# Transposing by DMA through DRAM instead of on the TensorE, in a kernel that gates two attention branches

## The chip, the cores and the metric

One core of a Trainium2 chip. The metric is the device time of one execution in microseconds (us). PE is TensorE, PEld its weight loads, DVE VectorE, ACT ScalarE, POOL GpSimd, and SP the engine that issues the DMAs. L12 is line 12 of the kernel that is being talked about, so the same statement has different line numbers in different kernels.

## The reference, cut to what matters

The input x has 2048 rows of 640. The output is `g * a + (1 - g) * b`, where g is a sigmoid of x times a vector, and a and b are two attention branches with 32 heads of 20.

```python
# branch A: linear attention; phi_k, phi_q are softmaxes of k, q times a small matrix
kv = einsum('bhsf,bhsd->bhfd', phi_k, v);  z = einsum('bhsf->bhf', phi_k)
a = (einsum('bhqf,bhfd->bhqd', phi_q, kv) / den) @ A_wo
# branch B: four segments of 512 rows; softmax attention inside a segment, memory M of earlier ones
logits = einsum('bhqd,bhkd->bhqk', qs, ks) * scale + mask
a_dot  = einsum('bhqk,bhkd->bhqd', softmax(logits), vs)
o = g * a_mem + (1 - g) * a_dot
b = o @ B_wo
```

## The kernel before

The matmuls of this kernel contract over the partition axis of both operands, so three things have to stand transposed: x (for all projections), k of branch B (for the scores) and both branches' outputs (for the last matmuls). The kernel before does each on PE, as a matmul with an identity, into one of four shared PSUM buffers, and DVE copies it out.

```python
psw = ctx.enter_context(tc.tile_pool(name="psw", bufs=4, space=PSUM))   # the four shared buffers
...
def x_transpose(sc):                      # 16 chunks of 128 rows
    tp = wtile("xtp", BF16)               # a shared PSUM buffer
    for c in range(KC):                   # KC = 5
        nc.tensor.transpose(out=tp[:, c * P:(c + 1) * P],
                            in_=x_nat[sc // 4][:, sc % 4, c * P:(c + 1) * P], identity=ident_b)
    nc.vector.tensor_copy(out=xT[:, :, sc * P:(sc + 1) * P], in_=...)
...
def b_kT(s, g):                           # segment s, group g of four heads: 32 times
    ps = wtile("kT_ps", BF16)
    for c in range(4):
        nc.tensor.transpose(out=ps[:, c * P:(c + 1) * P],
                            in_=kpad2[s % 2][:, c, 4 * g:4 * g + 4, :], identity=ident_b)
    kT = bw.tile([P, L], BF16, name="kT", bufs=2)
    nc.vector.tensor_copy(out=kT, in_=ps[:, 0:L])
    return kT
...
def fin_tr(s, qc, X):                     # X = 0: A's output, 1: B's; 32 times
    tp = wtile("otp", BF16)
    ...                                   # five transposes, one DVE copy to oT
def fin_mm(s, qc, hf):                    # ten matmuls oT x Wo, an ACT copy, at hf = 1 a DMA out
```

The kernel has three stages: branch A's keys and state over 16 chunks; a loop over 4 x 8 groups of heads; and a tail for the last segment's outputs. In the loop, a group's score matmuls (`st`), their exponentials on ACT (`PT`), and the previous group's value matmuls (`nd_ps`) are joined by filler units: next segment's k and v, branch A's outputs, and the output matmuls of earlier segments. Each unit has a fixed place in PE's order, given in groups:

```python
for s, (p0, p1) in enumerate(((9.01, 17), (17.01, 25), (25.4, 32))):   # output units of segment s
    fill += place(fill_fin(s), ((0, p0), (1, p1)))
```

The softmax here doesn't subtract the row's maximum and nothing guards it: scores larger than these inputs give would overflow.

## Time and profile before

| | before |
|---|---|
| median time, 16 executions | 438.92 us (436.54 to 441.15) |
| PE busy, share of the profiled span | 364.8 us of 436.2 us, 84% |
| ACT, DVE, POOL busy | 63%, 60%, 48% |
| loop, from the first to the last score matmul | 101.6 to 412.3 us |

First the page of the profiled execution before: the span; busy time, share and instruction count of each engine; the TensorE clock in tenths of full speed in 40 slices; the DMA totals; and the shares of the chain of work that ended last.

```profile
span 436.2 us, 10502 instructions
...
PE 364.8 (84%) x4289; PEld 234.1 (54%) x4289; DVE 260.2 (60%) x680; ACT 274.8 (63%) x515; POOL 210.6 (48%) x365
...
PEclk9999999999899798699999999899999997998669
...
DMA packets 10610, 12.49 MB, mean 29 GB/s; under 512 B 1347, under 2 KB 10563, under 8 KB 10563
...
PE 51%; ACT 19%; DVE 15%; POOL 9%; issue 4%; DMA 2%; POOLq 0%; SPq 0%; DVEq 0%; ACTq 0%
```

PE leads: it has the largest busy share and half of the chain. But the chain also passes through ACT, DVE and POOL, so PE is not the only thing that matters. Next, busy time of each engine in two stretches: ten microseconds of the first stage, and the whole loop. After the five busy times come the mean granted TensorE clock, the DMA share and GB/s.

```profile
core 0: us, PE busy (x) PEld busy (x) DVE busy (x) ACT busy (x) POOL busy (x), PEclk, DMA share, GB/s
40.00:50.00 10.00, 10.00 (x143) 8.24 (x142) 6.93 (x11) 5.84 (x17) 8.65 (x12) 1.00 0.01 3
101.60:412.30 310.70, 259.09 (x3112) 153.57 (x3114) 183.30 (x533) 216.89 (x365) 142.82 (x253) 0.93 0.02 7
```

In the first stage PE is busy without a gap. In the loop it is busy 259 of 310.7 us. In the 51.6 us that are left PE does nothing; most of that is waits. The clock is 0.93 on average. Next, the groups of the transposes and of one of the copies (busy us and mean ns after the first bar; then the idle time just before them and what ended it), and two rows of the timeline: five transposes' weight loads, and those of the next five matmuls.

```profile
L415 DVE COPY kT<-kT_ps 128x512 bf16<-128x512 bf16 x32 | 13.3, 416 | 0.9 <-PE kT_ps L412 0.9
...
L412 PE MATMUL kT_ps<-ident_b,kpad 128*128 128x128 bf16 x128 | 12.7, 221 | 1.8 <-DVE ts L538 0.9 <-ACT eq L401 0.9
...
L210 PE MATMUL xtp<-ident_b,x_nat 128*128 128x128 bf16 x80 | 8.0, 242 | 9.7 <-DVE xT L213 5.1 <-DMA x_nat<-in_A_x_dram 4.7
L551 PE MATMUL otp<-ident_b,oB 128*128 128x128 bf16 x80 | 7.8, 229 | 4.7 <-POOL oB L491 1.8 <-ACT eq L401 1.8 <-DVE ts L538 0.9
...
L551 PE MATMUL otp<-ident_b,oA 128*128 128x128 bf16 x80 | 7.6, 230 | 0.0
```

```profile
43.56 0.40 PEld L210 LDWEIGHTS <-x_nat 128*128 128x128 bf16 x5
...
43.92 0.36 PEld L184 LDWEIGHTS <-wnat_q 128*120 128x120 bf16 x5
```

One transpose is recorded as 220 ns long, but five of them take 43.92 - 43.56 = 0.36 us of PE's issue, 72 ns each, because they are pipelined. So busy time and issue time of the same instructions differ.

### The profile page before, as it was taken

To read this page: it belongs to the slowest core of one execution; us is meant where nothing else is said; L and a number is where in the kernel's file an instruction comes from. 1 tells how busy PE (TensorE), PEld (TensorE's weight loads), DVE (VectorE), ACT (ScalarE), POOL (GpSimd) and SP (SyncE) were. 2 spreads that over 40 slices of the span, in tenths; PEclk is the share of its full clock that TensorE was granted. 3 is DMA by queue.
4 is the path that set the end of the run, shared out by engine and by line. 5 is a ranking of instruction groups with operands and counts; after the bars stand their busy time and mean duration, and the time that the engine had idled before them with its cause. 6 is when DMAs were issued, how large, how long until landed. Compare 5 with 4: busy or idle time off the path is not lost.

```text
span 436.2 us, 10502 instructions
## 1 busy us (share of the span) xinstructions
PE 364.8 (84%) x4289; PEld 234.1 (54%) x4289; DVE 260.2 (60%) x680; ACT 274.8 (63%) x515; POOL 210.6 (48%) x365
## 2 busy tenths in 40 slices
PE   1899999797987687888988798898887788878686
PEld 1677877673544353455655465564554454445354
DVE  5378766795367454577666557565666556555431
ACT  1576666526687477677776776586675886676502
POOL 9037877860255434444453434454354544446510
PEclk9999999999899798699999999899999997998669
DMA  8961000000000000000000000000000000000001
GB/s 251 363 198 36 5 2 2 2 0 2 2 2 1 2 2 0 2 2 2 17 9 9 17 15 4 2 17 2 17 16 2 17 2 17 17 2 15 17 12 50
DMA packets 10610, 12.49 MB, mean 29 GB/s; under 512 B 1347, under 2 KB 10563, under 8 KB 10563
## 3 DMA queue, kind: packets, MB, share of 16 engines
q1 hardware_dynamic: 10563, 11.83, 8.3%
q8 instruction: 33, 0.54, 0.5%
q14 instruction: 14, 0.11, 0.1%
HBM read 9.21 MB, written 2.62 MB: 27 GB/s over the span
## 4 chain that ended last, share of the span: by engine, by line
PE 51%; ACT 19%; DVE 15%; POOL 9%; issue 4%; DMA 2%; POOLq 0%; SPq 0%; DVEq 0%; ACTq 0%
ACT PT L434 12%; PE o_ps L565 10%; PE pq_ps L500 6%; PE qb_ps L393 5%; PE st L428 4%; PE va_ps L231 4%; PE vb_ps L231 4%; PE nd_ps L448 4%; POOL PT L438 3%; PE kb_ps L231 3%; PE ka_ps L231 3%; DVE ts L538 2%; PE acc L271 2%; ACT eq L401 2%; PE otp L551 2%
## 5 line engine op out<-in xcount | busy, mean ns | idle before, releaser
L434 ACT ACTIVATE PT<-st 128x1024 bf16<-128x1024 f32 (+1 forms) x192 | 158.9, 885 | 21.0 <-PE st L428 18.7
L438 POOL TENSOR_SCALAR_AFFINE_SELECT PT<-PT 128x512 bf16<-128x512 bf16 x128 | 80.5, 641 | 113.4 <-ACT PT L434 97.8
L231 PEld LDWEIGHTS <-xT 128*128 128x128 bf16 x640 | 61.1, 99 | 31.6 <-issue 6.8
L428 PE MATMUL st<-qT,kT 32*128 32x128 bf16 (+3 forms) x512 | 44.6, 312 | 15.3 <-ACT PT L434 13.1
L397 DVE CAST qT<-qb_ps 128x512 bf16<-128x512 f32 x32 | 22.1, 692 | 45.6 <-PE qb_ps L393 45.6
L259 POOL TENSOR_TENSOR EkN<-Ek,krec 128x1280 bf16<-128x1280 bf16 x16 | 37.8, 2363 | 20.1 <-DVE krec L258 17.9
L448 PE MATMUL nd_ps<-vB,PT 128*128 128x21 bf16 x1280 | 42.5, 174 | 5.4 <-DVE ts L538 2.0
L448 PEld LDWEIGHTS <-PT 128*128 128x128 bf16 x1280 | 38.2, 96 | 11.7 <-POOL rr L529 3.8
L543 POOL TENSOR_TENSOR oA<-ts 128x360 bf16<-128x360 f32 (+1 forms) x32 | 27.5, 860 | 31.6 <-DVE ts L538 28.1
L393 PE MATMUL qb_ps<-xT,WqB 128*128 128x512 bf16 x160 | 41.7, 393 | 0.9 <-DVE ts L538 0.8
L500 PE MATMUL pq_ps<-xT,WqA 128*128 128x512 bf16 x120 | 35.0, 429 | 6.7 <-DVE ts L538 3.1
L565 PEld LDWEIGHTS <-oT 128*128 128x128 bf16 x320 | 31.6, 104 | 15.8 <-issue 1.7
L569 ACT CAST osb<-o_ps 128x320 bf16<-128x320 f32 x32 | 13.6, 425 | 40.1 <-PE o_ps L565 39.9
L428 PEld LDWEIGHTS <-kT 32*128 32x128 bf16 x512 | 14.0, 92 | 42.4 <-issue 37.1
L503 ACT ACTIVATE Eq<-pq_ps 128x512 bf16<-128x512 f32 x24 | 14.3, 597 | 29.4 <-PE pq_ps L500 29.2
L565 PE MATMUL o_ps<-WoA,oT 128*128 128x320 bf16 x160 | 30.2, 324 | 2.1 <-DVE ts L538 1.4
L518 PE MATMUL num_ps<-KVZ,Eq 128*128 128x132 bf16 (+1 forms) x192 | 18.5, 220 | 13.7 <-DVE ts L538 5.5
L231 PE MATMUL vb_ps<-WvB,xT 128*128 128x320 bf16 x160 | 26.5, 313 | 3.7 <-DVE ts L538 2.3
L565 PE MATMUL o_ps<-WoB,oT 128*128 128x320 bf16 x160 | 29.5, 319 | 0.0
L538 DVE TENSOR_TENSOR ts<-num_ps,cs 128x360 f32<-128x360 f32 (+1 forms) x64 | 28.2, 483 | 1.9 <-DVE cs L533 0.2
L241 ACT CAST vA<-va_ps 128x320 bf16<-128x320 f32 x32 | 13.6, 425 | 22.8 <-PE va_ps L231 22.8
L251 ACT ACTIVATE Ek<-ka_ps 128x320 bf16<-128x320 f32 x64 | 23.0, 440 | 5.5 <-PE ka_ps L231 4.9
(114 smaller groups left out, 667.0 us busy)
## 6 DMA issues: line engine op xcount, KB each, us to landing
out_dram<-osb SPq DMA_DIRECT2D x16, 160.0 KB, 1.8
x_nat<-in_A_x_dram SPq DMA_DIRECT2D x3, 640.0 KB, 8.9
WvA<-in_A_wqkv_dram SPq DMA_DIRECT2D x1, 800.0 KB, 5.3
wnat_k<-in_A_wqkv_dram SPq DMA_DIRECT2D x1, 800.0 KB, 7.0
wnat_q<-in_A_wqkv_dram SPq DMA_DIRECT2D x1, 800.0 KB, 11.0
WkB<-in_B_wk_dram SPq DMA_DIRECT2D x1, 800.0 KB
WvB<-in_B_wv_dram SPq DMA_DIRECT2D x1, 800.0 KB, 11.2
wq_st<-in_B_wq_dram SPq DMA_DIRECT2D x5, 160.0 KB, 7.7
```

The lines of the kernel that those rows point to most:

```text
L231: nc.tensor.matmul(ps, lhsT=xT[:, c, sc * P:(sc + 1) * P], rhs=W[:, c, lo:hi], start=(c == 0), stop=(c == KC - 1))
L251: nc.scalar.activation(out=Ek[:, sgn, 320 * hf:320 * hf + 320], in_=ps[:, 0:320], func=ACT.Exp, scale=1.0 if sgn == 0 else -1.0)
L259: nc.gpsimd.tensor_tensor(out=EkNs[sc % 4][:, 0:1280].rearrange("p (h f) -> p h f", f=DH), in0=Ek.rearrange("p s (h f) -> p (s h) f", f=DH ...
L393: nc.tensor.matmul(ps, lhsT=WqB[:, c, 4 * g:4 * g + 4, :], rhs=xT[:, c, s * L:(s + 1) * L], start=(c == 0), stop=(c == KC - 1))
L428: nc.tensor.matmul(st2[i // 2][:, i % 2, o:o + n], lhsT=kT[r:r + 32, c * P:(c + 1) * P], rhs=qT[r:r + 32, c * P:L], start=True, stop=True, ...
L434: nc.scalar.activation(out=PT[:, 2 * pr:2 * pr + 2, base:base + w], in_=st2[pr][:, :, 0:w], func=ACT.Exp, scale=SCALE_B)
L438: nc.gpsimd.affine_select(out=view, in_=view, pattern=[[0, 4], [1, P]], compare_op=ALU.is_ge, fill=0.0, base=0, channel_multiplier=-1)
L448: nc.tensor.matmul(nd[:, j * 84 + i * V1:j * 84 + (i + 1) * V1], lhsT=PT[:, i, o:o + P], rhs=vb[:, c, 4 * g + i, :], start=(j == 0 and i = ...
L500: nc.tensor.matmul(ps, lhsT=WqA[:, c, g * 120:g * 120 + P], rhs=xT[:, c, s * L:(s + 1) * L], start=(c == 0), stop=(c == KC - 1))
L538: nc.vector.tensor_tensor(out=ts[:, sgn, 0:nh, :], in0=pss[sgn][:, :, 0:DH], in1=cs[:, sgn, 0:nh, None].to_broadcast([P, nh, DH]), op=ALU. ...
L543: nc.gpsimd.tensor_tensor(out=segs[s].oA[:, qc, h0 * DH:(h0 + nh) * DH].rearrange("p (h d) -> p h d", d=DH), in0=ts[:, 0, 0:nh, :], in1=ts ...
L565: nc.tensor.matmul(ps[:, 0:320], lhsT=segs[s].oT[qc, X][:, k5 * P:(k5 + 1) * P], rhs=Wo[:, k5, hf * 320:hf * 320 + 320], start=(n == 0), s ...
```

## The change

Its intent is to take transposes off PE and their copies off DVE, and to use the DMA engines, which do almost nothing after the loads (share 0.01 to 0.02 above). Chunks 8 to 15 of x come by a transposing DMA straight from the input. k and the outputs are written to DRAM and read back by a transposing DMA. Only the last segment's B outputs stay on PE, as they would be waited for. Every one of these DMAs is issued by SP. The output units of each segment also start later in the loop, by 0.4 to 0.8 group. The core of the diff:

```diff
+    dram = ctx.enter_context(tc.tile_pool(name="dram", bufs=1, space=bass.MemoryType.DRAM))
+    kd = [dram.tile([L, H * 32], BF16, name=f"kd{s}") for s in range(NSEG)]
+    od = [[dram.tile([L, D], BF16, name=f"od{s}_{X}") for X in range(2)] for s in range(NSEG)]
...
-    for i in range(1, 4):
-        nc.sync.dma_start(out=x_nat[i], in_=xv[:, 4 * i:4 * i + 4, :])
+    nc.sync.dma_start(out=x_nat[1], in_=xv[:, 4:8, :])
     wload(wnat_q, A_wqkv[:, 0:D])
     wload(WkB, B_wk)
     wload(WvB, B_wv)
...                                              (five loads of B_wq, now into five buffers, not two)
+    for sc in range(8, NCH):
+        nc.sync.dma_start_transpose(out=xT[:, :, sc * P:(sc + 1) * P],
+                                    in_=x2[sc * P:(sc + 1) * P, :])
     wload(WoA, A_wo)
     wload(WoB, B_wo)
     nc.sync.dma_start(out=beta_b, in_=B_beta.partition_broadcast(P))
...                                              (in b_k: kpad is now three rotating tiles)
+        rows = slice(c * P, (c + 1) * P)
+        nc.sync.dma_start(out=kd[s][rows, :], in_=kp.rearrange("p h d -> p (h d)"))
+        nc.sync.dma_start_transpose(out=kT2[s % 2][:, :, rows], in_=kd[s][rows, :])
...                                              (b_kT is gone)
+    def o_put(s, X, qc, src):
+        nc.sync.dma_start(out=od[s][X][qc * P:(qc + 1) * P, :], in_=src)
+    def o_get(s, X, qc):
+        rows = slice(qc * P, (qc + 1) * P)
+        oT = bw.tile([P, KC, P], BF16, name=f"oT{X}", bufs=4)
+        nc.sync.dma_start_transpose(out=oT, in_=od[s][X][rows, :])
+        segs[s].oT[qc, X] = oT
...
-    for s, (p0, p1) in enumerate(((9.01, 17), (17.01, 25), (25.4, 32))):
-        fill += place(fill_fin(s), ((0, p0), (1, p1)))
+    for s, (p0, p1) in enumerate(((9.8, 17.2), (17.8, 25.2), (25.8, 32))):
+        fin = place(fill_fin(s), ((0, p0), (1, p1)))
+        fill += fin
+        for X in range(2):
+            fill += [(max(fin[2 * qc][0] - 0.8, 8 * s + 8.7),
+                      lambda s=s, X=X, qc=qc: o_get(s, X, qc)) for qc in range(4)]
```

## The prediction

> What bounds the kernel now. The page gives PE 364.8 us of 436.2 us (84%), ACT 63%, DVE 60%, POOL 48%. By windows there are three stages. From 20 to 80 us (branch A) PE is busy 9.5 to 10.0 us of every 10: it alone is the limit. From 100 to 400 us (the loop over 32 head groups) PE is busy 85 to 89%, ACT about 70%, DVE about 64%; the chain of work that ended last hops between PE matmuls, the ACT exponentials into PT and some DVE and POOL steps. PE leads, with small waits on others. The last 20 us are one chain: epilogue, transposes, output matmuls. DMA is nearly idle after 45 us.
>
> What the change removes. PE transposes: 40 of x (chunks 8 to 15), all 128 of k, 140 of 160 of the outputs: 308 of 4289 matmuls. By the groups of instructions these are 4.0 + 12.7 + 13.5 = 30 us of PE busy time. In the timeline five transposes in a row start 72 ns apart, so as issue time they are 308 x 72 ns = 22 us: 3 us in the PE-bound first stage, 19 us later. Also removed: copies out of PSUM on DVE, 8 x 0.49 + 32 x 0.42 + 28 x 0.49 = 31 us of DVE's 260 us, and 68 uses of the four shared PSUM buffers.
>
> What it adds. 44 writes to DRAM (160 to 256 KB) and 52 transposing DMAs, all issued by SP. In the trace a 160 KB output write lands in 1.8 us; it has no transposing DMA. The Trainium skill, "Advanced Engine Details and Errata", section "X-Bar Transpose (TRN2)", says that transposing DMAs on trn2 are as fast as regular ones; no run here shows that yet. My estimate is 2 us each, with 4 us allowed for. A write and its transpose are then 4 to 6 us of latency, in a queue that waits in order. The traffic is spread over 300 us. ACT and POOL work is unchanged.
>
> Critical path. k and A's outputs have lead times of several to tens of us (one group lasts about 10 us). Tight places: the last k chunk of segment 0 (its matmul ends near 97.7 us, its transpose is needed near 105.5 us), the first output chunk of each segment, and the eight x transposes, which queue behind about 6 MB of loads (estimate: done by 45 us, needed near 50 us). I allow 3 to 5 us of new PE waits there. The rest of the 22 us should show, since PE leads, plus a little from relieved DVE and PSUM.
>
> Predicted: 417 us, range 404 to 431. Faster by over 2%: 0.80; within 2%: 0.13; slower: 0.07.
>
> What would show it right. PE instructions down by 308 and PE busy to about 335 us; DVE to about 230 us; idle time of PE released by a DMA (kT, oT or xT) under 6 us in all; transposing DMAs landing within 2 to 4 us; the 20 to 80 us stage shorter by 3 us and the loop by 15 to 20 us.
>
> What would make it wrong. (a) Transposing DMAs far slower than plain ones, or slow to issue on SP, so that the queue becomes the limit: PE then waits for kT, oT or xT, and the time may exceed 437 us. (b) Head-of-line waits: a write whose data is late holds back a transpose that PE needs. (c) The loop is really paced by ACT and the handover of score buffers, so removed PE work turns into PE idle time: gain under 10 us. (d) A lower granted TensorE clock (now 0.945) with denser work.

## The result, and the profile after

| | before | after |
|---|---|---|
| median time | 438.92 us (16 executions) | 415.48 us (412.91 to 418.05, 11 executions) |
| ratio of mean times | | 0.9465 (95%: 0.9435 to 0.9495) |
| PE instructions | 4289 | 3981 |
| PE busy | 364.8 us | 349.6 us |
| DVE busy | 260.2 us | 234.7 us |
| first score matmul | 101.6 us | 98.6 us |
| loop | 310.7 us | 293.3 us |
| from the last score matmul to the end | 23.9 us | 23.7 us |

A ratio here, and in the experiments, is the mean time of one kernel's fast executions over that of the kernel before in the same rounds, so it is not quite the ratio of the medians. The result is as predicted: 5.35% faster, 1.5 us below the predicted time. The profiled execution after took 417.35 us and had the lowest clock of the kernel's twelve, 0.934 where their mean is 0.946. So the two profiles differ by 20.6 us only: 3.0 us before the loop, 17.4 in it, 0.2 after it. The page after:

```profile
span 415.6 us, 9989 instructions
...
PE 349.6 (84%) x3981; PEld 218.6 (53%) x3981; DVE 234.7 (56%) x612; ACT 273.2 (66%) x515; POOL 208.3 (50%) x366
...
PEclk9999999989899979799999988989998899999669
...
DMA packets 56977, 30.04 MB, mean 72 GB/s; under 512 B 43107, under 2 KB 54883, under 8 KB 56931
...
PE 43%; ACT 20%; POOL 10%; DVE 9%; DMA 6%; SPq 5%; issue 4%; POOLq 0%; DVEq 0%; ACTq 0%
```

PE lost 308 instructions, but only 15.2 us of busy time, and its share stayed at 84%. The DMAs moved 30 MB instead of 12.5, and packets under 512 B rose from 1347 to 43107. The same stretches as before (columns as there):

```profile
40.00:50.00 10.00, 10.00 (x131) 8.16 (x130) 5.59 (x10) 7.23 (x21) 8.49 (x16) 1.00 0.01 4
98.60:391.90 293.30, 245.91 (x2869) 141.37 (x2869) 164.79 (x478) 216.26 (x367) 141.21 (x250) 0.93 0.25 60
```

The loop lost 310.7 - 293.3 = 17.4 us. Of that, 259.1 - 245.9 = 13.2 us are PE busy time and 51.6 - 47.4 = 4.2 us are PE waits (called so for short: all time in which PE is idle). Three more microseconds went before the loop. Now the new DMAs: tiles, count, size (not given for the transposing ones) and median microseconds from issue to landing; then SP's own timeline (start, duration); then, of the tile that holds the transposed outputs, the SP instructions and the wait that PE and its weight loads had for them (us, times).

```profile
kd<-kpad SPq DMA_DIRECT2D x16, 256.0 KB, 2.2
od<-oA SPq DMA_DIRECT2D x16, 160.0 KB, 1.8
...
oT<-od SPq DMA_TRANSPOSE x28, 2.9
kT<-kd SPq DMA_TRANSPOSE x16, 3.2
xT<-in_A_x_dram SPq DMA_TRANSPOSE x8, 3.5
```

```profile
15.19 13.19 SPq L114 DMA_TRANSPOSE xT<-in_A_x_dram  x8
...
29.63 0.52 SPq L118 DMA_DIRECT2D beta_b<-in_B_beta_dram  x1
...
148.60 0.33 SPq L554 DMA_DIRECT2D od<-oA  x1
151.17 1.20 SPq L559 DMA_TRANSPOSE oT<-od  x1
```

```profile
L559 SPq DMA_TRANSPOSE oT<-od x28: 1198/1202/2062, 151.2 to 395.2; - x28
...
  DMA oT<-od: 1.7, 3
```

A transposing DMA keeps SP for 1.20 us against 0.33 us for a write, and lands in 2.9 to 3.2 us against 1.8 to 2.2 us. Part of that is reading against writing: in the run plain_dma below the same reads, not transposed, landed in 2.3 us (`oT`) and 3.2 us (`kT`) and kept SP for 0.35 and 0.53 us, where the transposing ones keep it for 1.20 and 1.23 us. The eight transposes of x held SP for 13.19 us, and the small load of beta, last in program order, went out only at 29.63 us. PE and its weight loads waited for transposed outputs for 1.7 us in all, three times (PE itself once, 0.5 us), and for kT and xT never.

So the forecast total is there. Whether it is there for the forecast reason is another question: busy time was to fall by 30 us, and the forecast counted on 72 ns of PE issue for each removed transpose. The experiments ask this.

### The profile page after: what moved, and what is told of

The parts are those of the page before. It is cut to its first block, busy times and chain, and to the rows that moved or that the text cites. A ratio compares the mean times of both kernels' runs of the same rounds, so it can differ in the third digit from the quotient of the medians.

```text
span 415.6 us, 9989 instructions
## 1 busy us (share of the span) xinstructions
PE 349.6 (84%) x3981; PEld 218.6 (53%) x3981; DVE 234.7 (56%) x612; ACT 273.2 (66%) x515; POOL 208.3 (50%) x366
## 4 chain that ended last, share of the span: by engine, by line
PE 43%; ACT 20%; POOL 10%; DVE 9%; DMA 6%; SPq 5%; issue 4%; POOLq 0%; DVEq 0%; ACTq 0%
ACT PT L436 13%; PE o_ps L579 10%; PE qb_ps L404 6%; PE pq_ps L504 4%; POOL PT L440 4%; PE st L430 4%; PE vb_ps L239 3%; PE kb_ps L239 3%; DMA WvB<-in_B_wv_dram 3%; PE va_ps L239 3%; PE ka_ps L239 3%; DVE ts L542 2%; PE nd_ps L450 2%; PE acc L279 2%; SPq L114 2%
## 5 line engine op out<-in xcount | busy, mean ns | idle before, releaser
L436 ACT ACTIVATE PT<-st 128x1024 bf16<-128x1024 f32 (+1 forms) x192 | 158.7, 887 | 19.7 <-PE st L430 16.4
L430 PE MATMUL st<-qT,kT 32*128 32x128 bf16 (+3 forms) x512 | 47.2, 312 | 19.1 <-ACT PT L436 17.0
L404 PE MATMUL qb_ps<-xT,WqB 128*128 128x512 bf16 x160 | 44.1, 410 | 1.9 <-DVE ts L542 1.9
L450 PEld LDWEIGHTS <-PT 128*128 128x128 bf16 x1280 | 37.0, 96 | 14.6 <-issue 8.9
L430 PEld LDWEIGHTS <-kT 32*128 32x128 bf16 x512 | 15.2, 92 | 47.5 <-issue 44.5
L583 ACT CAST osb<-o_ps 128x320 bf16<-128x320 f32 x32 | 13.6, 426 | 38.4 <-PE o_ps L579 37.9
L504 PE MATMUL pq_ps<-xT,WqA 128*128 128x512 bf16 x120 | 33.4, 414 | 1.9 <-DVE ts L542 0.9
L239 PE MATMUL vb_ps<-WvB,xT 128*128 128x320 bf16 x160 | 27.6, 320 | 2.7 <-DVE ts L542 0.9
L479 DVE RECIPROCAL rd<-nd_ps 128x16 f32<-128x16 f32 x32 | 8.0, 249 | 36.1 <-PE nd_ps L450 35.9
L249 ACT CAST vA<-va_ps 128x320 bf16<-128x320 f32 x32 | 13.5, 426 | 20.4 <-PE va_ps L239 20.4
L239 PE MATMUL kb_ps<-WkB,xT 128*128 128x320 bf16 x160 | 26.1, 309 | 1.0 <-ACT eq L412 1.0
```

Of the source, the lines that this page charges most:

```text
L239: nc.tensor.matmul(ps, lhsT=xT[:, c, sc * P:(sc + 1) * P], rhs=W[:, c, lo:hi], start=(c == 0), stop=(c == KC - 1))
L404: nc.tensor.matmul(ps, lhsT=WqB[:, c, 4 * g:4 * g + 4, :], rhs=xT[:, c, s * L:(s + 1) * L], start=(c == 0), stop=(c == KC - 1))
L430: nc.tensor.matmul(st2[i // 2][:, i % 2, o:o + n], lhsT=kT[r:r + 32, c * P:(c + 1) * P], rhs=qT[r:r + 32, c * P:L], start=True, stop=True, ...
L436: nc.scalar.activation(out=PT[:, 2 * pr:2 * pr + 2, base:base + w], in_=st2[pr][:, :, 0:w], func=ACT.Exp, scale=SCALE_B)
L450: nc.tensor.matmul(nd[:, j * 84 + i * V1:j * 84 + (i + 1) * V1], lhsT=PT[:, i, o:o + P], rhs=vb[:, c, 4 * g + i, :], start=(j == 0 and i = ...
L504: nc.tensor.matmul(ps, lhsT=WqA[:, c, g * 120:g * 120 + P], rhs=xT[:, c, s * L:(s + 1) * L], start=(c == 0), stop=(c == KC - 1))
```

## The experiments

Four theories are told apart. Theory 1 (the prediction's): PE leads, so each removed transpose gives its 72 ns. Rival 2: the gain is the relief of DVE and of the shared PSUM buffers. Rival 3: the gain is the new place of the output units. Rival 4: the queue of transposing DMAs costs some of the gain. In the table, microseconds are (1 - ratio) x 438.5 us, the mean of the kernel before in these rounds (438.6 and 438.45); the clock is the mean granted clock over a kernel's executions (before: 0.941). There are six executions of each kernel, but twelve of the changed one, five of pe_back and four of plain_dma. The runs were made in three sets on three chips, so two of them are compared through the kernel before, which ran in each set.

| run | ratio (95%) | median us | against before, us | clock |
|---|---|---|---|---|
| changed kernel | 0.9465 (0.9435 to 0.9495) | 415.48 | -23.5 | 0.946 |
| x_only | 0.9946 (0.9905 to 0.9987) | 435.90 | -2.4 | 0.943 |
| xk | 0.9762 (0.9725 to 0.9799) | 427.95 | -10.4 | 0.937 |
| o_only | 0.9854 (0.9812 to 0.9896) | 432.39 | -6.4 | 0.937 |
| xo | 0.9814 (0.9767 to 0.9862) | 431.58 | -8.2 | 0.935 |
| place_only | 0.9997 (0.9946 to 1.0049) | 437.98 | -0.1 | 0.949 |
| pe_back | 0.9531 (0.9502 to 0.9559) | 417.12 | -20.6 | 0.953 |
| dve_back | 0.9535 (0.9499 to 0.9572) | 417.03 | -20.4 | 0.945 |
| pe_copy_back | 0.9839 (0.9807 to 0.9871) | 431.45 | -7.1 | 0.931 |
| plain_dma | 0.9403 (0.9378 to 0.9428) | 411.97 | -26.2 | 0.946 |
| after_oldplace | 0.9866 (0.9828 to 0.9904) | 431.96 | -5.9 | 0.921 |
| beta_early | 0.9397 (0.9367 to 0.9427) | 412.19 | -26.4 | 0.949 |
| more_dma | 0.9367 (0.9336 to 0.9398) | 410.44 | -27.8 | 0.945 |

### One part at a time: x_only, xk, o_only, place_only, xo

These are the kernel before with the hunks of one or two parts of the diff above. k alone was not run; it was tried on top of x.

```diff
 x_only      before + the x hunks (x_nat, wq_st bufs 5, eight transposing DMAs, sc + 4 < 8)
 xk          before + the x hunks + the k hunks (kd, kT2, b_k; b_kT removed)
 o_only      before + the output hunks and the new places
 xo          changed kernel with b_kT and the old b_k back
 place_only  before, and only:
-    ((9.01, 17), (17.01, 25), (25.4, 32))
+    ((9.8, 17.2), (17.8, 25.2), (25.8, 32))
```

> The kernel before with the x part alone: chunks 8 to 15 of x transposed by DMA, 40 PE transposes and 8 DVE copies fewer. Theory 1 (PE issue time, 72 ns for each removed transpose, because PE leads): 40 x 72 ns = 2.9 us faster, all of it in the stage before the loop. Rival 2 (the relief of DVE and of the shared PSUM buffers makes the gain): in this stage PE is busy all the time, so nothing beyond the PE time; under 1.5 us if the DMA transposes collide with the loads.

> The x part and the k part, the outputs still transposed on PE at the old places. Theory 1: x 2.9 us plus k 128 x 72 ns = 9.2 us, so about 12 us faster than the kernel before. Rival 2 (DVE and PSUM relief): k also removes 13.3 us of DVE copies and 32 uses of a PSUM buffer, so 15 us or more. Rival 3 (the gain is the new places of the output units): 3 us at most.

> The output part alone with its new places: 140 PE transposes and 28 DVE copies fewer. Theory 1: 140 x 72 ns = 10.1 us faster. Rival 3 (places): as large a gain, but then the run that only moves the places shows it as well. If parts add up, this and the run with x and k together give the whole 23 us.

> The kernel before with nothing changed but the places of the output units in the loop (each segment's units start 0.4 to 0.8 group later). Theory 1: within 1.5 us of the kernel before. Rival 3: 5 us faster or more.

> The changed kernel with k's transposes back on PE (x and output parts kept). Theory 1 (issue time): 128 x 72 ns = 9.2 us slower than the changed kernel, near 425 us. If parts help one another (the whole gives 5.35%, the parts summed give 3.84%): 11 us or more, near 427 us.

Measured: x gives 2.4 us (forecast 2.9; by the interval 0.6 to 4.2), and in its profile the loop starts 2.8 us earlier. That fits Theory 1, but Rival 2 forecast the same here. The places alone give nothing, so Rival 3 falls. x with k gives 10.4 us where 12 were forecast, the outputs 6.4 us where 10.1 were forecast. But the parts do not add up. x with k and the outputs alone sum to 16.8 us, the whole is 23.5 us. k is worth 10.4 - 2.4 = 8.0 us on top of x, but 23.5 - 8.2 = 15.3 us on top of x and the outputs. A fixed 72 ns per transpose, and nothing else, can't do that.

### PE time alone, DVE time alone, and both joined by a PSUM buffer

All three add idle work to the changed kernel: pe_back and pe_copy_back at the place where k's transposes were, dve_back two copies in each group.

```diff
 pe_back: 31 x 4 transposes, nobody reads them
+            if t == 1 and k + 1 < NG:
+                dm = wtile("dm_ps", BF16)
+                for c in range(4):
+                    nc.tensor.transpose(out=dm[:, c * P:(c + 1) * P],
+                                        in_=WoA[:, c, 0:P], identity=ident_b)
 pe_copy_back: these, and also
+                dsb = bw.tile([P, L], BF16, name="dsb", bufs=1)
+                nc.vector.tensor_copy(out=dsb, in_=dm[:, 0:L])
 dve_back: in the changed kernel, two copies per group, no transposes
+            if t < 2:
+                dm = bw.tile([P, 400], BF16, name="dm", bufs=1)
+                nc.vector.tensor_copy(out=dm, in_=Msrc)      # 400 f32 values of a constant tile
```

> The changed kernel plus four idle PE transposes in each of 31 groups at the place where the k transposes were, into a PSUM buffer that nobody reads, no DVE copy: 124 transposes return as PE time alone. Theory 1: 124 x 72 ns = 8.9 us slower than the changed kernel, about 424 us. Rival 2 (DVE and PSUM relief): under 3 us slower.

> The changed kernel plus two idle DVE copies of 400 elements per partition in each of 32 groups, about 0.4 us each, 26 us of DVE time in all, nobody waits for them: nearly the DVE time that the change removed. Theory 1: under 3 us slower than the changed kernel. Rival 2: 10 us slower or more.

> The changed kernel plus the four idle PE transposes per group as before, and now a DVE copy of 512 columns out of their PSUM buffer into a tile that nobody reads: PE time, DVE time and a shared PSUM buffer held until DVE gets to it, but no consumer. PE time alone gave 2.9 us, DVE time alone 3.1 us. If the two only add: 6 us slower than the changed kernel. If the held PSUM buffer is what k's transposes cost: 8 us or more. If only a consumer that waits makes the cost: 3 us.

Measured, against the changed kernel: the transposes alone cost 2.9 us, a third of what Theory 1 said. But the clock rose with them: its mean is 0.953 against 0.946, and the lowest of the five executions (0.951) lies above the highest of the changed kernel's twelve (0.950). So 2.9 us is not yet the price of the PE time; the next table takes this apart. DVE time alone costs 3.1 us; DVE's busy time rose by 23.7 us in its profile. Both joined by the PSUM buffer cost 16.4 us, more than five times the transposes alone and far over the sum of 6. Nobody reads what they make, so it isn't a consumer that waits. What is new is that a PSUM buffer, one of four, is held until DVE gets round to the copy. This returns as much time as k's real transposes (xo: 15.3 us). Both theories' forms of a simple sum fall.

Where did the 13.5 us between pe_back and pe_copy_back go? The whole loop, with PE's transposes alone and then with transposes and copies (columns as before):

```profile
97.10:392.60 295.50, 249.37 (x2995) 147.33 (x2994) 165.79 (x478) 216.55 (x367) 140.70 (x250) 0.95 0.24 59
```

```profile
98.70:407.20 308.50, 258.06 (x2995) 150.59 (x2994) 175.50 (x509) 216.75 (x367) 141.02 (x250) 0.92 0.22 57
```

PE executes the same 2995 matmul records in both. The loop grew by 13.0 us. PE's waits grew from 46.1 to 50.4 us, so 4.3 us. The other 8.7 us are the same instructions being busy longer, and the clock column says why: 0.95 became 0.92. In these traces the clock is 1.00 or 0.50 and nothing between, so the stretches at half rate can be picked out and summed. Here are the sums over them in the loop, before, after, in pe_back and in pe_copy_back (us at half rate, then the busy times inside; the means can be passed over):

```profile
sum 40.77, PE 35.19 PEld 16.28 DVE 15.39 ACT 16.52 POOL 24.71; mean PE 4.40 PEld 2.04 DVE 1.92 ACT 2.07 POOL 3.09
sum 40.97, PE 38.10 PEld 18.32 DVE 17.21 ACT 19.94 POOL 23.44; mean PE 4.23 PEld 2.04 DVE 1.91 ACT 2.22 POOL 2.60
sum 31.76, PE 28.49 PEld 13.84 DVE 15.73 ACT 13.95 POOL 15.82; mean PE 4.07 PEld 1.98 DVE 2.25 ACT 1.99 POOL 2.26
sum 51.80, PE 47.10 PEld 23.35 DVE 21.97 ACT 22.05 POOL 26.13; mean PE 4.71 PEld 2.34 DVE 2.20 ACT 2.21 POOL 2.61
```

PE was busy at half rate for 18.6 us more with the copies. At full rate that work would take half the time, so about 9.3 us were lost, near the 8.7.

The same sums give an estimate of PE's work: its busy time in the loop, with the part at half rate counted half.

| profile | loop, us | PE busy | of that at half rate | PE work (estimate) | PE waits |
|---|---|---|---|---|---|
| before | 310.7 | 259.1 | 35.2 | 241.5 | 51.6 |
| changed kernel | 293.3 | 245.9 | 38.1 | 226.9 | 47.4 |
| pe_back | 295.5 | 249.4 | 28.5 | 235.1 | 46.1 |
| pe_copy_back | 308.5 | 258.1 | 47.1 | 234.5 | 50.4 |
| xo | 308.3 | 257.4 | 45.8 | 234.5 | 50.9 |
| xk | 302.1 | 251.9 | 37.9 | 232.9 | 50.2 |
| o_only | 304.6 | 253.5 | 37.5 | 234.8 | 51.1 |

place_only, whose loop has the same instructions as the kernel before, comes to 243.1 us by this estimate, so differences under 2 us mean little. Three things are read from it.

- The 124 idle transposes of pe_back did add 8.2 us of PE work, near Theory 1's 8.9. Of it, 4.8 us were paid back by 9.6 us less of busy time at half rate, and 1.3 us by shorter waits. That is one profile each, but the higher clock is in all five executions.
- PE's work adds up: k takes away 8.6 us, the outputs 6.7, both together 14.6, which is 60 ns for each of the 244 transposes removed from the loop (four of k lie before it, 20 of the last outputs after it). What does not add up in these profiles is the waits: they fall by 1.4 us with x and k, by 0.5 with the outputs, and by 4.2 with all. Over the executions it is the clock: 0.937, 0.937 and 0.946. And xk lost some 2 us before the loop to a wait for beta (below).
- k's transposes on PE (xo against the changed kernel) cost 15.0 us of loop: 7.6 us of PE work, 3.5 us of waits, and 7.7 us more at half rate, which lose 3.9.

A place where a wait goes with a slow clock is found where the two runs pass the same point of the program. First PE's timeline with the transposes alone (start, duration; in brackets the idle time before and its releaser), then with the copies:

```profile
194.57 0.34 PE L522 MATMUL num_ps<-KVZ,Eq 128*128 128x132 bf16 x3 [1.01 <-ACT eq L412]
...
195.46 0.75 PE L450 MATMUL nd_ps<-vB,PT 128*128 128x21 bf16 x24
196.07 0.84 PE L239 MATMUL vb_ps<-WvB,xT 128*128 128x320 bf16 x5
197.14 0.84 PE L239 MATMUL vb_ps<-WvB,xT 128*128 128x320 bf16 x5 [0.23 <-DVE ts L542]
```

```profile
199.47 0.33 PE L522 MATMUL num_ps<-KVZ,Eq 128*128 128x132 bf16 x3 [1.01 <-ACT eq L412]
...
200.35 0.75 PE L450 MATMUL nd_ps<-vB,PT 128*128 128x21 bf16 x24
202.04 2.29 PE L239 MATMUL vb_ps<-WvB,xT 128*128 128x320 bf16 x8 [0.93 <-DVE ts L542]
```

Both wait 1.01 us for ACT. Then the run without copies starts `vb_ps` at once, and its second half after 0.23 us. The run with copies waits 0.93 us for a buffer that DVE has yet to release, by the copies `ts`. DVE was not late with them. In both runs they start 1.98 to 1.99 us after `num_ps`, as DVE's rows show (first without, then with copies):

```profile
196.56 0.97 DVE L542 TENSOR_TENSOR ts<-num_ps,cs 128x360 f32<-128x360 f32 x2
...
201.45 0.97 DVE L542 TENSOR_TENSOR ts<-num_ps,cs 128x360 f32<-128x360 f32 x2
```

So it looks as if one free buffer was missing: that of the idle transposes, whose copy comes only after `ts`. In the whole run PE waited 0.9 us for such a copy itself, twice; the rest of the 4.3 us are waits put down to other DVE work. That the held buffer is the cause is therefore inferred. No run changes the number of shared buffers alone, and the copy also ties DVE's order to PE's, since DVE waited 3.4 us in all for these transposes. Here is what follows in that run, in windows of one microsecond (PE busy is the second number, the clock the third from the end):

```profile
199.00:200.00 1.00, 0.53 (x11) 0.27 (x10) 0.83 (x5) 0.58 (x2) 0.62 (x1) 1.00 0.92 210
200.00:201.00 1.00, 1.00 (x36) 0.93 (x29) 0.76 (x3) 0.86 (x2) 0.50 (x2) 1.00 0.41 162
201.00:202.00 1.00, 0.10 (x5) 0.03 (x2) 0.80 (x3) 1.00 (x2) 0.00 (x0) 0.90 0.02 6
202.00:203.00 1.00, 0.96 (x4) 0.55 (x4) 0.76 (x2) 0.10 (x1) 0.50 (x1) 0.50 0.08 23
...
204.00:205.00 1.00, 1.00 (x5) 0.45 (x4) 0.16 (x2) 0.00 (x0) 0.61 (x2) 0.50 0.38 83
205.00:206.00 1.00, 1.00 (x5) 0.44 (x4) 0.39 (x1) 0.00 (x0) 0.00 (x0) 0.89 0.00 0
```

In the second of two gaps of about 1 us the clock drops to 0.50, at 201.8 us, and stays there for 3.4 us, while PE is almost fully busy. In the 3.4 us before the drop PE was idle for 1.7 us. In the other run the same eight microseconds have a clock of 1.00 throughout. The pattern holds beyond this place. In the loops of all 14 profiles the clock falls 120 times, in each profile only at points of one fixed grid of 3.41 us. In the grid interval before each fall PE was idle for 0.79 us or more, and each interval at full rate with more than 1.45 us of idle time was followed by a fall; between the two figures both happen. So it also counts whether two gaps lie in the same interval. The Trainium skill, "TensorE: Matmul & The Clock Gate", section "A second HAM failure mode: psum-queue depth-cycling", tells of this: a kernel whose PE stops briefly between groups while PSUM buffers are cycled lets the clock gate swing between half and full rate. This trace agrees, with the numbers above.

So transposes whose PSUM buffer waits for a busy DVE have three costs: their PE work, the waits, and then microseconds at half rate. That also fits that parts are worth more together, at least in kind: whether a further wait tips the clock may depend on the other waits near it. Why xo's clock fell just so far is not shown; its executions fell into two groups, two at 426.6 and 427.8 us with a clock of 0.940, and four at 431 to 433 us with 0.929 to 0.933.

### The queue: plain_dma and after_oldplace

```diff
 plain_dma: all 52 transposing DMAs of the changed kernel become plain ones of the same bytes, e.g.
-        nc.sync.dma_start_transpose(out=oT, in_=od[s][X][rows, :])
+        nc.sync.dma_start(out=oT, in_=od[s][X][rows, :].rearrange("p (c k) -> p c k", k=P))
 after_oldplace: changed kernel, old places; reads come as early as the data allow
-    ((9.8, 17.2), (17.8, 25.2), (25.8, 32))      max(fin[2 * qc][0] - 0.8, 8 * s + 8.7)
+    ((9.01, 17), (17.01, 25), (25.4, 32))        max(fin[2 * qc][0] - 0.8, 8 * s + 9.0)
```

> The changed kernel with each of the 52 transposing DMAs replaced by a plain DMA of the same bytes to the same tile; the result is wrong on purpose. It shows what the transposing form itself costs (issue on SP 1.2 us instead of 0.33 us, landing 2.9 to 3.2 us). Theory 1 (the queue is off the critical path): within 2 us of the changed kernel. Rival 4 (the queue's length costs some of the gain): 4 us faster or more.

> The changed kernel with the output units at their old places, so the first output matmuls of a segment come about 0.1 group after the write of its last outputs instead of about 0.8. Theory 1 with a write and a transpose of about 6 us in sequence: PE waits for oT by DMA some 4 to 6 us in each of three segments, 8 to 18 us slower than the changed kernel. If the old places were as good, within 2 us.

Measured: without transposing (a wrong result) the kernel is 2.7 us faster. That lies between the two forecasts, so the transposing form costs something small. With the old places it is 17.6 us slower, at the upper end of the forecast. The wait for the outputs is there in its profile (total us, times, longest):

```profile
PE o_ps L579 <- DMA oT<-od: 7.0, 3, 2.8
```

These three waits explain 7.0 us. In its profile 2.4 us more are lost before the loop, which starts at 101.0 us; the next section says why. The clock again takes a share: its mean is 0.921 against 0.946, the lowest of all runs. Thus the later places, worth nothing by themselves, are what lets the DMA latency hide.

### A small load stuck behind the transposes: beta_early

In the lead-in to the loop the profiles of xk and after_oldplace lost 2 to 3 us that the changed kernel's did not. The reason is the 8 KB load of beta. ACT's timeline of the changed kernel, then of after_oldplace, and a PE row of the changed kernel:

```profile
35.87 0.23 ACT L358 ACTIVATE sig_b<-beta_b 128x32 f32<-128x32 bf16 x1 [2.15 <-DMA beta_b<-in_B_beta_dram]
36.00 0.67 ACT L196 COPY WTq<-wtp 120x640 bf16<-120x640 bf16 x1
```

```profile
38.38 0.23 ACT L358 ACTIVATE sig_b<-beta_b 128x32 f32<-128x32 bf16 x1 [5.05 <-DMA beta_b<-in_B_beta_dram]
```

```profile
36.73 0.84 PE L239 MATMUL ka_ps<-WkA,xT 128*128 128x320 bf16 x5 [0.38 <-ACT WTq L196]
```

ACT's next instruction, a copy, starts only after the one that reads beta (36.00 after 35.87 us), and PE waits for that copy: 0.38 us here, 3.3 us in after_oldplace. In the kernel before, that load didn't hold ACT up.

```diff
     nc.sync.dma_start(out=x_nat[1], in_=xv[:, 4:8, :])
+    nc.sync.dma_start(out=beta_b, in_=B_beta.partition_broadcast(P))
     wload(wnat_q, A_wqkv[:, 0:D])
...
-    nc.sync.dma_start(out=beta_b, in_=B_beta.partition_broadcast(P))     # after WoA, WoB
```

> The changed kernel with one 8 KB load (beta) issued before the third weight load instead of behind the eight transposes of x and two weight loads. In the changed kernel and its variants the ACT instruction that reads beta waits 1.5 to 5.1 us for it, and PE then waits 0.4 to 3.3 us for the ACT copy queued behind it. If that is a real cost of the new queue: 1 to 3 us faster than the changed kernel, and no wait for beta. If it is noise: within 0.5 us.

Measured: 3.0 us faster than the changed kernel, and the wait is gone:

```profile
15.82 0.23 ACT L358 ACTIVATE sig_b<-beta_b 128x32 f32<-128x32 bf16 x1
```

In the profiles the loop starts 1.0 us earlier, and the rest lies in the loop, where this profile spent less time at half rate (clock 0.95 against 0.93 over the loop). So 1 us or so is the wait itself; the rest is not tied to it by any run. plain_dma had no wait for beta either, and its gain is of the same size, so Rival 4's cost may be nothing but this.

### More of the same: more_dma

```diff
 beta_early, and
-    wload(wnat_q, A_wqkv[:, 0:D])
+    WTq = apool.tile([P, NG6, KC, P], BF16, name="WTq")
+    for g in range(NG6):                                   # after the transposes of x
+        nc.sync.dma_start_transpose(out=WTq[:, g].rearrange("p c k -> p (c k)"),
+                                    in_=A_wqkv[:, g * 120:g * 120 + P])
-            fold_tr(fq, sc - 3)                            # 30 PE transposes, 6 copies
```

> The early beta load, and also the 30 PE transposes of A's query weights by DMA (six transposing DMAs of 160 KB in place of one load of 800 KB; three ACT and three DVE copies go too). 30 x 72 ns = 2.2 us in the stage where PE is busy all the time. Theory 1: 2 us faster than the run with the early beta load alone, some 3 to 4 us faster than the changed kernel. If the added transposes delay the other loads: no faster than the early beta load alone.

Measured: 410.44 us, with a right result. It beats both kernels, the changed one by (0.9465 - 0.9367) x 438.5 = 4.3 us. Against beta_early it is 1.3 us, and the intervals overlap, so that the further transposes help is not resolved.

## Why the prediction was right

The time (417 us forecast, 415.48 us measured) and the direction were right. Point by point:

- "PE leads" and the first stage: right. The loop starts 3.0 us earlier, as forecast, and x alone gives 2.4 us for 40 transposes, where 72 ns each would be 2.9 us. The loop is 17.4 us shorter, where 15 to 20 were forecast.
- "308 x 72 ns = 22 us": the main term, right in kind and a little too large. In the loop PE's work fell by an estimated 14.6 us where 244 x 72 ns = 17.6 us would be due, and the time at half rate was the same in both profiles (40.8 and 41.0 us). With the 3.0 us before the loop that is 17.6 us. Put back as idle work, 124 transposes added 8.2 us of PE work (8.9 forecast), though only 2.9 us of time, as the clock rose.
- "3 to 5 us of new PE waits" and "a little from relieved DVE and PSUM": these are the terms that were mis-sized. PE's waits did not grow, they fell by 4.2 us; new ones for the DMAs were 1.7 us at most. Transposes with a DVE copy of their PSUM buffer cost 16.4 us in a kernel that had lost them, without it 2.9. That the too large first term and this too small one made up for each other, so that the time came within 1.5 us, is partly luck.
- "PE busy to about 335 us": wrong, it was 349.6 us. The recorded 220 ns of a transpose overlap what comes before and after, so 30 us of busy time in the groups were never 30 us of PE's time. The profiled execution also had a clock of 0.934 against 0.945.
- "DVE to about 230 us": 234.7 us. "Transposing DMAs landing within 2 to 4 us": medians of 2.9 to 3.5 us, the longest of `kT` 4.9. "PE idle released by a DMA under 6 us": 1.7 us. All held, but for the longest landings.
- "Transposing DMAs ... 2 us each", after the skill: too low, but inside the 4 us that were allowed for. The later places of the output units were needed for it; with the old ones 17.6 us of the gain are lost.
- Risk (b), a transpose held back in the queue: the one case was the other way round. A plain 8 KB load was held back by transposes. Moving it made the kernel 3.0 us faster, of which about 1 us is the wait itself.
- Risk (d), a lower clock with denser work: the mean clock was 0.946 after and 0.941 before. The runs point the opposite way: with more PE work and no more waits (pe_back) the clock rose to 0.953, with more waits (pe_copy_back) it fell to 0.931.

## What to carry to other kernels

Put back into the changed kernel, k's transposes cost 15.3 us where their issue time is 9.2 us: their PSUM buffer came from a small shared pool, and a busy engine had to empty it. So count the buffer as well as the 72 ns. Gaps of 1 us on PE went with several more at half clock here, so sum the time at half rate before you explain a difference of busy time, or of the whole time: pe_back seemed to show that 8.2 us of PE work cost 2.9 us. When work moves to a DMA queue, place its consumers later by the queue's latency, and send small loads that someone needs early ahead of the long ones.

## What the Trainium skill lacked or had wrong

- "Advanced Engine Details and Errata", section "X-Bar Transpose (TRN2)": it says that transposing DMAs on trn2 are as fast as regular ones and expects 350 to 400 GB/s. Here the landing came near that: 2.9 us for a transposing read of 160 KB and 3.2 us for one of 256 KB, against 2.3 and 3.2 us for the plain reads of plain_dma. But the transposing DMA of 160 KB held SP for 1.20 us against 0.35 us, which alone limits a row of them to an estimated 160 KB / 1.20 us = 137 GB/s. This page gives no time on the issuing engine.
- "TensorE: Matmul & The Clock Gate", section "Part 1: The HAM clock gate": its table has the clock fall to half after at least one idle window of about 3.4 us. Here the clock fell after 3.4 us in which PE was idle for 1.7 us only, in two gaps with work between them, and half rate then lasted 3.4 us. Of all 120 falls in the loops the least idle time before one was 0.79 us. The section on psum-queue depth-cycling of the same page has it right in kind, but gives no length of gap.
- No page that I found says what a PSUM buffer held for a copy costs: 16.4 us for 31 times four transposes with their copies, where the transposes alone cost 2.9 us, at a higher clock.
